# Key-value products of an attention kernel on 64x64 quarters of the array

## The chip, the cores and the metric

The kernel runs on one core of one Trainium2 chip. The metric is the device time of one execution in microseconds. Three executions of the kernel before took 288.51, 288.64 and 288.70 us; their median is 288.64.

## The reference

Eight batches of eight heads, 576 positions, head size 64, go through a linear attention: queries and keys each get a softmax of their own, keys and values are multiplied first, and a two-layer network follows.

```python
q_s = softmax(q, over the 64 features)
k_s = softmax(k, over the 576 positions)
kv  = einsum('bhsd,bhse->bhde', k_s, v)
a   = einsum('bhsd,bhde->bhse', q_s, kv)
x   = a, heads joined             # 4608 x 512
h   = x @ w_in                    # 512 x 2048
out = maximum(0.01 * h, h) @ w_out   # 2048 x 512
```

## The kernel before, in words

The 4608 rows are cut into nine tiles of 512 rows (`t` = 0 to 8), and the network runs tile by tile. For each tile `layer1` (L474) multiplies the transposed attention output `xT` by `w_in`, `leaky` (L483, ScalarE) writes the activations `gj`, `layer2` (L495) multiplies them by `w_out`, and `store` (L489) copies the result out and sends it. These matmuls use the whole array, 128 rows by 128 columns.

The attention of a batch is prepared while the network of earlier tiles runs. There is no scheduler: the order on each engine is the order of the program text. Small steps are hung on places of the network's loops by `at(t, u, ...)` and issued there by `run(t, u)`. So PE (TensorE) meets a batch's key-value products and its attention products at fixed places between the matmuls of the network. In stage 0, up to about 26 us, the steps for batch 0 are written out one after another, with `wake` matmuls of zeros between them, and PE has little else to do.

For one batch a tile of 128 partitions holds two heads at once: the partition number is 64 times the head's parity (`hh`) plus the block of positions, and each partition holds nine positions (`r` = 0 to 8) of four heads, `h` = 0 to 3 (`HL`). Thus every product over positions is a sum of nine matmuls with 64 rows each.

`v_cast` (L203 on ScalarE, L205 on GpSimd) writes the values as bf16 into `vb2`, beside a column of ones; the product of the keys' exponentials with that column is the sum by which the softmax of the keys is divided. `k_exp` writes the exponentials to `ke`.

`kv` (L287, batches 1 to 7) and `kv_pair` (L362, batch 0, in two halves) multiply. One matmul takes two heads at a time (`gg` is the pair): 64 rows, 128 columns of weights (two heads of 64 features), and 129 moving columns (two heads of 64 values, and the ones). Its output is 128 by 129, of which the two diagonal 64x64 blocks and the last column are used. The two parities `hh` are on the upper and the lower 64 rows of the array and write to different banks.

`kd_make` (L302 and L305) and, for batch 0, `kd_rec` (L373) and `kd_one` (L380) take the reciprocal of the sums and multiply the blocks with it into `kd2`, on VectorE, with one operation for each 64 partitions (`hp`), since the two blocks stand in different columns:

```python
for hp in range(2):
    rows = slice(hp * D, (hp + 1) * D)
    nc.vector.tensor_scalar(
        out=kd2[b % 2][rows, 2 * hh + gg],
        in0=pkv[rows, hp * D : (hp + 1) * D],
```

`quads` (L423), called by `attend` and `attend_x`, then multiplies the queries with `kd2` on 64x64 quarters of the array, and `move` copies the result to `xT` (L414, L416). The queries of batch 0 are turned by PE (`q_transpose`, L392, after `q_norm`, L272); those of later batches by a DMA (`q_turn`).

Of the kernel before, what the change touches and what calls it, by code (L numbers as in the profile page):

```python
# [8 lines left out]
FP32 = mybir.dt.float32  # L9
BF16 = mybir.dt.bfloat16  # L10
AF = mybir.ActivationFunctionType
ALU = mybir.AluOpType
# [7 lines left out]
L = 64  # L20
R = 9
HL = 4
# [3 lines left out]
def kernel(  # L26
# [9 lines left out]
    nc = tc.nc  # L36
# [3 lines left out]
    B, H, S, D = q.shape  # L40
# [6 lines left out]
    P = 128  # L47
# [7 lines left out]
    const_pool = ctx.enter_context(tc.tile_pool(name="const", bufs=1))  # L55
# [11 lines left out]
    psB_pool = ctx.enter_context(tc.tile_pool(name="psB", bufs=6, space=bass.MemoryType.PSUM))  # L67
    psO_pool = ctx.enter_context(tc.tile_pool(name="psO", bufs=2, space=bass.MemoryType.PSUM))
    BANK_TAG = "bank2k"


    def load(src, b, name, cuts):
# [15 lines left out]
    st = [{} for _ in range(B)]  # L88
# [7 lines left out]
        out=st[0]["q"][:, :, RB].rearrange("p h r d -> p h (r d)"),  # L96
        in_=qflat[:, :, RB].rearrange("p h r d -> p h (r d)"),
# [13 lines left out]
    w_out_sb = w_pool.tile([P, NF, O], BF16)  # L111
    xT = xT_pool.tile([P, NB, T], BF16)

    vb2 = [const_pool.tile([P, R, 2, 130], BF16, name=f"vb{i}") for i in range(2)]
    kd2 = [const_pool.tile([P, NB, D], BF16, name=f"kd{i}") for i in range(2)]
    for i in range(2):
        nc.gpsimd.memset(vb2[i][:, :, :, 128:129], 1.0)


    w_in_r = moe_w_in.rearrange("(c p) f -> p c f", p=P)  # L120
# [76 lines left out]
        )  # L197

    def v_cast(eng, b, gg):
        o = vb2[b % 2][:, :, gg, 0:128].rearrange("p r (h d) -> p h r d", h=2)  # L200
        i = st[b]["v"][:, 2 * gg : 2 * gg + 2]
        if eng is nc.scalar:
            eng.copy(out=o, in_=i)  # L203
        else:
            eng.tensor_copy(out=o, in_=i)  # L205
# [71 lines left out]
        )  # L277


    def kv(b):  # L280

        pkv = [psB_pool.tile([P, 2, 130], FP32, name="pkv", tag=BANK_TAG) for _ in range(2)]
        for gg in range(2):
            for r in range(R):
                for hh in range(2):
                    rows = slice(hh * L, (hh + 1) * L)
                    nc.tensor.matmul(  # L287
                        pkv[hh][:, gg, 0:129],
                        lhsT=st[b]["ke"][rows, r, 2 * gg : 2 * gg + 2].rearrange(
                            "p h d -> p (h d)"  # L290
                        ),
                        rhs=vb2[b % 2][rows, r, gg, 0:129],
                        start=(r == 0),
                        stop=(r == R - 1),
                    )
        st[b]["pkv"] = pkv

    def kd_make(b):
        for hh in range(2):
            pkv = st[b]["pkv"][hh]  # L300
            krec = small_pool.tile([P, 2, 1], FP32, name="krec")
            nc.vector.reciprocal(out=krec, in_=pkv[:, :, 128:129])  # L302
            for hp in range(2):
                p0 = hp * D
                nc.vector.tensor_tensor(  # L305
                    out=kd2[b % 2][p0 : p0 + D, 2 * hh : 2 * hh + 2],
                    in0=pkv[p0 : p0 + D, :, p0 : p0 + D],
                    in1=krec[p0 : p0 + D].to_broadcast([D, 2, D]),
                    op=ALU.mult,
                )  # L310

    wake_ps = psO_pool.tile([P, TT], FP32, name="pout")

# [41 lines left out]
        )  # L355

    def kv_pair(b, gg):
        pkv = [psB_pool.tile([P, 130], FP32, name="pkv1", tag=BANK_TAG) for _ in range(2)]
        for r in range(R):
            for hh in range(2):  # L360
                rows = slice(hh * L, (hh + 1) * L)
                nc.tensor.matmul(  # L362
                    pkv[hh][:, 0:129],
                    lhsT=st[b]["ke"][rows, r, 2 * gg : 2 * gg + 2].rearrange("p h d -> p (h d)"),
                    rhs=vb2[b % 2][rows, r, gg, 0:129],
                    start=(r == 0),
                    stop=(r == R - 1),
                )
        st[b]["pkv", gg] = pkv

    def kd_rec(b, gg, hh):
        st[b]["krec", gg, hh] = krec = small_pool.tile([P, 1], FP32, name="krec1")
        nc.vector.reciprocal(out=krec, in_=st[b]["pkv", gg][hh][:, 128:129])  # L373

    def kd_one(b, gg, hh):

        pkv, krec = st[b]["pkv", gg][hh], st[b]["krec", gg, hh]
        for hp in range(2):
            rows = slice(hp * D, (hp + 1) * D)
            nc.vector.tensor_scalar(  # L380
                out=kd2[b % 2][rows, 2 * hh + gg],
                in0=pkv[rows, hp * D : (hp + 1) * D],
                scalar1=krec[rows],
                scalar2=None,
                op0=ALU.mult,
            )

    def q_transpose(b, r0, n):
        ps = psB_pool.tile([P, NB, n, L], BF16, name="psum_qt", tag=BANK_TAG)
# [159 lines left out]
    k_exp(0, slice(0, 1))  # L549
    nc.gpsimd.tensor_copy(out=gate[:, 0:1], in_=st[0]["k"][:, 0, R - 1, D - 1 : D])  # L550
    v_cast(nc.gpsimd, 0, 1)
    k_all_dve(0, 1)
    k_all_pe(0, 1)
    wake(5)
    k_sub_ps(0, 0, HB)
    k_exp(0, slice(1, 2))
    v_cast(nc.scalar, 0, 0)
    k_sub_ps(0, 1)
    nc.gpsimd.tensor_copy(out=gate[:, 0:1], in_=st[0]["k"][:, HL - 1, R - 1, D - 1 : D])
    load_w_in(8, 16)  # L560
    k_exp(0, H1)
    q_first_rec(0, RA)
    q_norm(0, RA)
    kv_pair(0, 0)
    wake(1)
    q_transpose(0, 0, 4)
    kv_pair(0, 1)
    for hh in range(2):
        kd_rec(0, 0, hh)
        kd_one(0, 0, hh)  # L570
# [4 lines left out]
    q_sub(nc.gpsimd, 0, R1)  # L575
    q_keep(nc.vector, 0, 0, 4, (1,))
    kd_rec(0, 1, 0)
    kd_rec(0, 1, 1)
    kd_one(0, 1, 0)
    kd_one(0, 1, 1)  # L580
    q_exp(0, R1)
    q_max(0, R2)
# [18 lines left out]
    at(0, 15, lambda: k_sub(nc.vector, 1, H0), lambda: k_sub(nc.vector, 1, H1))  # L601
    at(0, 15, lambda: q_max(1, XR[1]), lambda: q_sub(nc.gpsimd, 1, XR[1]))
    at(0, 31, lambda: q_exp(1, XR[0]), lambda: k_exp(1, H0), lambda: v_cast(nc.scalar, 1, 0))
    at(0, 31, lambda: k_exp(1, H1), lambda: v_cast(nc.scalar, 1, 1), lambda: q_exp(1, XR[1]))
    at(0, 31, lambda: q_sum(1, XR[0]), lambda: q_norm(1, XR[0]))
    at(0, 34, lambda: q_turn(1, XR[0]))
    at(0, 39, lambda: kv(1), lambda: q_sum(1, XR[1]), lambda: q_norm(1, XR[1]), lambda: kd_make(1))
    at(0, 43, lambda: q_turn(1, XR[1]), lambda: load_all(2))
    for i in range(2):
# [6 lines left out]
    def plan(b, o):  # L616
        t = b - 2
        at(t, o, lambda: k_begin(b), lambda: q_begin(b), lambda: k_tree(b, ALLH))
        at(t, o + 3, lambda: k_allmax(b), lambda: k_sub(nc.gpsimd, b, ALLH))
        at(t, o + 7, lambda: q_max(b, ALLR), lambda: q_sub(nc.gpsimd, b, ALLR))  # L620
        at(t, o + 11, lambda: k_exp(b, ALLH))
        at(t, o + 12, lambda: v_cast(nc.gpsimd, b, 0), lambda: v_cast(nc.gpsimd, b, 1))
        at(t, o + 16, lambda: q_exp(b, ALLR))
        at(t, o + 18, lambda: q_sum(b, ALLR))
        at(t, o + 21, lambda: q_norm(b, ALLR))
        kvu, pu = o + 25, o + (33 if b == 3 else 34)
        at(t, kvu, lambda: kv(b))
        at(t, kvu + 1, lambda: kd_make(b))
        at(t, o + 22, lambda: q_turn(b))
        at(t, pu + 1, lambda: attend_x(b, (0, 1), (nc.scalar,)))  # L630


    def plan2():
        b = 2
        at(1, 0, lambda: k_begin(b), lambda: q_begin(b), lambda: k_tree(b, ALLH))
        at(1, 3, lambda: k_allmax(b))
        at(1, 6, lambda: k_sub(nc.vector, b, H0), lambda: k_sub(nc.vector, b, H1))
        at(1, 12, lambda: k_exp(b, ALLH))
        for rs in XR:
            at(1, 9, lambda rs=rs: q_max(b, rs), lambda rs=rs: q_sub(nc.gpsimd, b, rs))  # L640
        at(1, 13, lambda: v_cast(nc.gpsimd, b, 0), lambda: v_cast(nc.gpsimd, b, 1))
        for i, rs in enumerate(XR):
            at(1, (15, 16)[i], lambda rs=rs: q_exp(b, rs), lambda rs=rs: q_sum(b, rs), lambda rs=rs: q_norm(b, rs))
            at(1, (16, 17)[i], lambda rs=rs: q_turn(b, rs))
        at(1, 23, lambda: kv(b))
        at(1, 24, lambda: kd_make(b))
        for i in range(2):
            at(1, 28 + 2 * i, lambda i=i: attend_x(b, (i,), (nc.scalar,)))
# [121 lines left out]
```

## Time and profile before

| | us |
|---|---|
| median of three runs | 288.64 |
| profiled execution | 288.82 |
| span of its instructions | 287.0 |
| PE busy | 278.5 |
| VectorE busy | 150.5 |
| ScalarE busy | 146.0 |
| GpSimd busy | 82.3 |
| matmuls of `kv`, L287, 252 of them | 8.4 |
| `kd_make`, L305, 28 operations | 8.1 |
| `kd_one`, L380, 8 operations | 2.3 |

The profile is of one execution. PE is the matmul side of TensorE and PEld its weight loads, which overlap the matmuls; DVE is VectorE, ACT ScalarE, POOL GpSimd, SP the engine that issues most DMAs. A row of the groups names line, engine, operation, output and inputs, shapes and count, then busy time and the mean length of one. The length of a matmul in the profile is modelled and contains its passage through the array; how fast matmuls follow each other is read from their starts. The granted clock of TensorE was 1.00 throughout.

### The profile page before, as it was taken

To read this page: it belongs to the slowest core of one execution; us is meant where nothing else is said; L and a number is where in the kernel's file an instruction comes from. 1 tells how busy PE (TensorE), PEld (TensorE's weight loads), DVE (VectorE), ACT (ScalarE), POOL (GpSimd) and SP (SyncE) were. 2 spreads that over 40 slices of the span, in tenths; PEclk is the share of its full clock that TensorE was granted. 3 is DMA by queue.
4 is the path that set the end of the run, shared out by engine and by line. 5 is a ranking of instruction groups with operands and counts; after the bars stand their busy time and mean duration, and the time that the engine had idled before them with its cause. 6 is when DMAs were issued, how large, how long until landed. Compare 5 with 4: busy or idle time off the path is not lost.

```text
span 287.0 us, 4376 instructions
## 1 busy us (share of the span) xinstructions
PE 278.5 (97%) x1706; PEld 134.5 (47%) x1706; DVE 150.5 (52%) x250; ACT 146.0 (51%) x262; POOL 82.3 (29%) x61
## 2 busy tenths in 40 slices
PE   7699999999999999999999999999999999999995
PEld 2266744454444444454454444444454444444443
DVE  2997886896970994498185727563621100110011
ACT  4957890586269308923674358434843065016400
POOL 2522661017059009504900590049100000000000
PEclk9999999999999999999999999999999999999999
DMA  7999997999859174953398239913141310130032
GB/s 249 322 211 332 284 178 142 393 302 381 152 117 399 61 155 110 402 142 77 81 388 182 63 82 352 227 41 80 27 85 37 73 37 2 44 80 23 2 73 73
DMA packets 38868, 46.35 MB, mean 161 GB/s; under 512 B 18240, under 2 KB 21568, under 8 KB 38848
## 3 DMA queue, kind: packets, MB, share of 16 engines
q1 hardware_dynamic: 35456, 41.75, 49.8%
q0 software_dynamic: 3232, 4.19, 8.3%
q8 instruction: 13, 0.21, 0.3%
q10 hardware_dynamic: 160, 0.13, 0.1%
q14 instruction: 7, 0.06, 0.1%
HBM read 36.70 MB, written 9.44 MB: 161 GB/s over the span
## 4 chain that ended last, share of the span: by engine, by line
PE 91%; DVE 4%; issue 0%; ACT 0%
PE pout L495 44%; PE ph L474 42%; PE pkv L287 3%; PE po L423 2%; DVE kd L380 1%; DVE k_raw L353 1%; DVE qe L272 1%; DVE qmax L217 1%; DVE q_raw L248 0%; PE psum_qt L392 0%; DVE qT L410 0%; DVE qsum L265 0%; ACT qT L408 0%; DVE krec L373 0%; DVE out_sb L489 0%
## 5 line engine op out<-in xcount | busy, mean ns | idle before, releaser
L495 PE MATMUL pout<-w_out_sb,gj 128*128 128x512 bf16 (+2 forms) x592 | 127.9, 373 | 0.0
L474 PE MATMUL ph<-xT,w_in_sb 128*128 128x512 bf16 (+3 forms) x640 | 127.3, 358 | 0.0
L483 ACT ACTIVATE gj<-ph 128x512 bf16<-128x512 f32 (+2 forms) x152 | 83.3, 579 | 55.1 <-PE ph L474 53.3
L474 PEld LDWEIGHTS <-w_in_sb 128*128 128x128 bf16 x640 | 62.2, 98 | 62.1 <-issue 0.5
L495 PEld LDWEIGHTS <-gj 128*128 128x128 bf16 x592 | 56.3, 98 | 66.4 <-issue 1.9
L489 DVE COPY out_sb<-pout 128x512 f32<-128x512 f32 (+1 forms) x34 | 22.7, 675 | 83.6 <-PE pout L495 78.0
L185 POOL TENSOR_TENSOR k_raw<-k_raw,kall 128x2304 f32<-128x2304 f32 x5 | 25.3, 5066 | 75.7 <-DVE kall L177 45.4
L414 ACT CAST xT<-po 128x320 bf16<-128x320 f32 (+2 forms) x45 | 18.0, 486 | 47.8 <-PE po L423 47.8
L265 DVE TENSOR_REDUCE qsum<-qe 128x36 f32<-128x2304 bf16 (+4 forms) x11 | 19.8, 1798 | 32.1 <-ACT qe L256 32.1
L248 POOL TENSOR_TENSOR q_raw<-q_raw,qmax 128x2304 f32<-128x2304 f32 (+3 forms) x10 | 29.7, 2973 | 22.2 <-DVE qmax L217 22.2
L193 ACT ACTIVATE ke<-k_raw 128x2304 bf16<-128x2304 f32 (+2 forms) x11 | 17.5, 1595 | 11.1 <-POOL k_raw L185 10.9
L272 DVE TENSOR_TENSOR qe<-qe,qrec 128x2304 bf16<-128x2304 bf16 (+4 forms) x12 | 21.9, 1826 | 0.4
L217 DVE TENSOR_REDUCE qmax<-q_raw 128x36 f32<-128x2304 f32 (+4 forms) x11 | 19.6, 1792 | 0.5 <-DMA q_raw<-in_q_dram 0.5
L256 ACT ACTIVATE qe<-q_raw 128x2304 bf16<-128x2304 f32 (+4 forms) x11 | 16.8, 1525 | 3.1 <-POOL q_raw L248 1.7
L205 POOL CAST vb<-v_raw 128x1152 bf16<-128x1152 f32 x13 | 14.6, 1147 | 0.0
L152 DVE TENSOR_TENSOR t<-k_raw 128x1024 f32<-128x1024 f32 (+1 forms) x10 | 10.1, 1011 | 0.5 <-DMA k_raw<-in_k_dram 0.2
L316 PE MATMUL pout<-zero 128*128 128x512 bf16 x28 | 9.0, 450 | 1.3 <-POOL zero L101 1.3
L152 DVE TENSOR_TENSOR t<-t 128x256 f32<-128x256 f32 (+2 forms) x20 | 9.6, 478 | 0.7
L489 ACT COPY out_sb<-pout 128x512 f32<-128x512 f32 (+1 forms) x3 | 1.6, 544 | 14.1 <-PE pout L495 14.1
L287 PEld LDWEIGHTS <-ke 64*128 64x128 bf16 x252 | 7.1, 93 | 3.0 <-ACT gj L483 1.7
L305 DVE TENSOR_TENSOR kd<-pkv,krec 64x128 bf16<-64x128 f32 x28 | 8.1, 289 | 0.8
L287 PE MATMUL pkv<-vb,ke 64*128 64x129 bf16 x252 | 8.4, 216 | 0.0
(55 smaller groups left out, 91.5 us busy)
## 6 DMA issues: line engine op xcount, KB each, us to landing
out_dram<-out_sb SPq DMA_DIRECT2D x70, 128.0 KB, 2.4
q_raw<-in_q_dram SPq DMA_DIRECT2D x7, 1152.0 KB, 8.8
v_raw<-in_v_dram SPq DMA_DIRECT2D x7, 1152.0 KB, 11.6
k_raw<-in_k_dram SPq DMA_DIRECT2D x6, 1152.0 KB, 5.9
k_raw<-in_k_dram SPq DMA_DIRECT2D x4, 576.0 KB, 5.8
w_in_sb<-in_moe_w_in_dram POOLq DMA_DIRECT2D x4, 512.0 KB, 7.6
v_raw<-in_v_dram SPq DMA_DIRECT2D x2, 576.0 KB, 7.6
w_out_sb<-in_moe_w_out_dram POOLq DMA_DIRECT2D x4, 256.0 KB, 9.1
```

The source lines that it names most:

```text
L152: nc.vector.tensor_tensor(out=o, in0=i0, in1=i1, op=ALU.max)
L185: eng.tensor_tensor(out=ks, in0=ks, in1=st[b]["kall"][:, hs].unsqueeze(2).to_broadcast([P, n, R, D]), op=ALU.subtract,)
L217: nc.vector.tensor_reduce(out=m, in_=st[b]["q"][:, :, rs], axis=AX.X, op=ALU.max)
L248: eng.tensor_tensor(out=qs, in0=qs, in1=st[b]["qmax", rs.start].unsqueeze(3).to_broadcast([P, HL, n, D]), op=ALU.subtract,)
L265: nc.vector.reduce_sum(out=qsum, in_=st[b]["qe"][:, rs], axis=AX.X)
L272: nc.vector.tensor_tensor(out=qes, in0=qes, in1=st[b]["qrec", rs.start].unsqueeze(3).to_broadcast([P, n, HL, D]), op=ALU.mult,)
L287: nc.tensor.matmul(pkv[hh][:, gg, 0:129], lhsT=st[b]["ke"][rows, r, 2 * gg : 2 * gg + 2].rearrange("p h d -> p (h d)"), rhs=vb2[b % 2][row ...
L414: eng.copy(out=o, in_=i)
L474: nc.tensor.matmul(ph, lhsT=w_in_sb[:, i, j * P : (j + 1) * P], rhs=xT[:, i, c0 : c0 + n], start=(i == 0 and first), stop=(i == NB - 1 and ...
L483: nc.scalar.activation(out=o, in_=ph, func=AF.Prelu, alpha=LEAKY_SLOPE)
L489: copy(out=out_sb, in_=pout)
L495: nc.tensor.matmul(pout, lhsT=g_sb[j // 2][:, j % 2, tsub * P : (tsub + 1) * P], rhs=w_out_sb[:, j, os], start=(j == 0), stop=(j == NF - 1),)
```

## The change

Each key-value matmul now takes one head: 64 rows, 64 columns of weights, and 65 moving columns (the head's 64 values and a column of ones of its own). The two heads of a pair go to the two halves of the output's partitions, so that four matmuls, one for each quarter of the array, belong to each `r` and pair. A product of four pairs of heads is 72 matmuls and 72 weight loads instead of 36 and 36. All sums lie in one column, and both blocks in the same 64 columns, so one VectorE operation on 128 partitions divides what took two on 64. The rest of the program keeps its order on every engine.

```diff
-    vb2 = [const_pool.tile([P, R, 2, 130], BF16, name=f"vb{i}") for i in range(2)]
+    vb2 = [const_pool.tile([P, R, HL, 66], BF16, name=f"vb{i}") for i in range(2)]
...
-        nc.gpsimd.memset(vb2[i][:, :, :, 128:129], 1.0)
+        nc.gpsimd.memset(vb2[i][:, :, :, D : D + 1], 1.0)
...
-        o = vb2[b % 2][:, :, gg, 0:128].rearrange("p r (h d) -> p h r d", h=2)
+        o = vb2[b % 2][:, :, 2 * gg : 2 * gg + 2, 0:D].rearrange("p r h d -> p h r d")
...
-    def kv(b):
-
-        pkv = [psB_pool.tile([P, 2, 130], FP32, name="pkv", tag=BANK_TAG) for _ in range(2)]
-        for gg in range(2):
-            for r in range(R):
-                for hh in range(2):
-                    rows = slice(hh * L, (hh + 1) * L)
+    def kv_half(b, gg, outs):
+
+        for r in range(R):
+            for hh in range(2):
+                rows = slice(hh * L, (hh + 1) * L)
+                for hp in range(2):
                     nc.tensor.matmul(
-                        pkv[hh][:, gg, 0:129],
-                        lhsT=st[b]["ke"][rows, r, 2 * gg : 2 * gg + 2].rearrange(
-                            "p h d -> p (h d)"
-                        ),
-                        rhs=vb2[b % 2][rows, r, gg, 0:129],
+                        outs[hh][hp * D : (hp + 1) * D],
+                        lhsT=st[b]["ke"][rows, r, 2 * gg + hp],
+                        rhs=vb2[b % 2][rows, r, 2 * gg + hp, 0 : D + 1],
                         start=(r == 0),
                         stop=(r == R - 1),
                     )
+
+    def kv(b):
+        pkv = [psB_pool.tile([P, 2, 66], FP32, name="pkv", tag=BANK_TAG) for _ in range(2)]
+        for gg in range(2):
+            kv_half(b, gg, [p[:, gg, 0 : D + 1] for p in pkv])
         st[b]["pkv"] = pkv
...
             krec = small_pool.tile([P, 2, 1], FP32, name="krec")
-            nc.vector.reciprocal(out=krec, in_=pkv[:, :, 128:129])
-            for hp in range(2):
-                p0 = hp * D
-                nc.vector.tensor_tensor(
-                    out=kd2[b % 2][p0 : p0 + D, 2 * hh : 2 * hh + 2],
-                    in0=pkv[p0 : p0 + D, :, p0 : p0 + D],
-                    in1=krec[p0 : p0 + D].to_broadcast([D, 2, D]),
-                    op=ALU.mult,
-                )
+            nc.vector.reciprocal(out=krec, in_=pkv[:, :, D : D + 1])
+            nc.vector.tensor_tensor(
+                out=kd2[b % 2][:, 2 * hh : 2 * hh + 2],
+                in0=pkv[:, :, 0:D],
+                in1=krec.to_broadcast([P, 2, D]),
+                op=ALU.mult,
+            )
...
     def kv_pair(b, gg):
-        pkv = [psB_pool.tile([P, 130], FP32, name="pkv1", tag=BANK_TAG) for _ in range(2)]
...
+        pkv = [psB_pool.tile([P, 66], FP32, name="pkv1", tag=BANK_TAG) for _ in range(2)]
+        kv_half(b, gg, [p[:, 0 : D + 1] for p in pkv])
         st[b]["pkv", gg] = pkv
...
     def kd_one(b, gg, hh):
 
-        pkv, krec = st[b]["pkv", gg][hh], st[b]["krec", gg, hh]
-        for hp in range(2):
-            rows = slice(hp * D, (hp + 1) * D)
-            nc.vector.tensor_scalar(
-                out=kd2[b % 2][rows, 2 * hh + gg],
-                in0=pkv[rows, hp * D : (hp + 1) * D],
-                scalar1=krec[rows],
-                scalar2=None,
-                op0=ALU.mult,
-            )
+        nc.vector.tensor_scalar(
+            out=kd2[b % 2][:, 2 * hh + gg],
+            in0=st[b]["pkv", gg][hh][:, 0:D],
+            scalar1=st[b]["krec", gg, hh],
+            scalar2=None,
+            op0=ALU.mult,
+        )
```

More of the change, by code (lines that the diff above doesn't have):

```diff
@@ L357, in kv_pair @@
     def kv_pair(b, gg):
-        pkv = [psB_pool.tile([P, 130], FP32, name="pkv1", tag=BANK_TAG) for _ in range(2)]
[L359 to L367, printed above, removed]
-                )
+        pkv = [psB_pool.tile([P, 66], FP32, name="pkv1", tag=BANK_TAG) for _ in range(2)]
+        kv_half(b, gg, [p[:, 0 : D + 1] for p in pkv])
         st[b]["pkv", gg] = pkv
@@ L372, in kd_rec @@
         st[b]["krec", gg, hh] = krec = small_pool.tile([P, 1], FP32, name="krec1")
-        nc.vector.reciprocal(out=krec, in_=st[b]["pkv", gg][hh][:, 128:129])
+        nc.vector.reciprocal(out=krec, in_=st[b]["pkv", gg][hh][:, D : D + 1])
     def kd_one(b, gg, hh):
-        pkv, krec = st[b]["pkv", gg][hh], st[b]["krec", gg, hh]
-        for hp in range(2):
-            rows = slice(hp * D, (hp + 1) * D)
-            nc.vector.tensor_scalar(
-                out=kd2[b % 2][rows, 2 * hh + gg],
-                in0=pkv[rows, hp * D : (hp + 1) * D],
-                scalar1=krec[rows],
-                scalar2=None,
-                op0=ALU.mult,
-            )
+        nc.vector.tensor_scalar(
[5 more added lines that the diff above has]
+        )
     def q_transpose(b, r0, n):
```

## The prediction

> **What bounds the kernel now.** I read the page first: TensorE (PE) is busy nearly the whole span, and the chain that ended last runs through PE for 91% of it.
>
> ```profile
> PE 278.5 (97%) x1706; PEld 134.5 (47%) x1706; DVE 150.5 (52%) x250; ACT 146.0 (51%) x262; POOL 82.3 (29%) x61
> ...
> PE 91%; DVE 4%; issue 0%; ACT 0%
> PE pout L495 44%; PE ph L474 42%; PE pkv L287 3%; PE po L423 2%; DVE kd L380 1%; DVE k_raw L353 1%; DVE qe L272 1%; DVE qmax L217 1%; DVE q_raw L248 0%; PE psum_qt L392 0%; DVE qT L410 0%; DVE qsum L265 0%; ACT qT L408 0%; DVE krec L373 0%; DVE out_sb L489 0%
> ```
>
> The change touches two entries of this chain: the key-value products of batches 1 to 7 (L287, 3%), and in stage 0 the division on VectorE (DVE kd L380, 1%). Time taken from PE between 26 and 283 us is time off the span; VectorE counts only where PE waits for it, and that is in stage 0.
>
> One product of a later batch, from PE's timeline at 97.7 to 99.7 us (start, length, operation, count):
>
> ```profile
> 98.45 1.20 PE L287 MATMUL pkv<-vb,ke 64*128 64x129 bf16 x36
> 99.58 0.39 PE L495 MATMUL pout<-w_out_sb,gj 128*128 128x512 bf16 x1
> ```
>
> 36 matmuls and 36 weight loads take 1.13 us from the first matmul to the next one of another kind. In the trace they start in twos, 3 ns apart (the upper and the lower 64 rows of the array), and the twos follow every 56 ns, about 129 columns at full clock; the last starts 0.985 us after the first. Then 0.15 us pass until the next 128-row matmul starts: 54 ns of streaming and a gap of 92 ns, which the trace shows at each change of tile shape (L423 to L495 too).
>
> The same 64x64 quarters that the change wants are already used by L423. Its rows in the window 107.45 to 107.47 us, and the whole group:
>
> ```profile
> 107.45 0.11 PEld L423 LDWEIGHTS <-kd 64*64 64x64 bf16 x4 [0.42 <-issue]
> 107.45 0.33 PE L423 MATMUL po<-qX,kd 64*64 64x320 bf16 x4
> ...
> 107.45 0.68 PE L423 MATMUL po<-qX,kd 64*64 64x320 bf16 x16
> 108.07 0.39 PE L495 MATMUL pout<-w_out_sb,gj 128*128 128x512 bf16 x1
> ```
>
> Four matmuls of four quarters start within 10 ns, and the next four 136 ns later, which is 320 columns: four quarters do run side by side. The second four of a group come another 14 ns late, waiting for their weights.
>
> Stage 0, VectorE and then PE, from the timeline at 14 to 25 us:
>
> ```profile
> 14.46 0.60 DVE L380 TENSOR_SCALAR kd<-pkv,krec 64x64 bf16<-64x64 f32 x2
> 15.09 0.17 DVE L373 RECIPROCAL krec<-pkv 128x1 f32<-128x1 f32 x1
> 15.29 0.60 DVE L380 TENSOR_SCALAR kd<-pkv,krec 64x64 bf16<-64x64 f32 x2
> ...
> 17.18 1.23 DVE L380 TENSOR_SCALAR kd<-pkv,krec 64x64 bf16<-64x64 f32 x4
> ...
> 17.65 0.29 PE L423 MATMUL po<-qT,kd 64*64 64x256 bf16 x1
> 18.14 0.62 PE L423 MATMUL po<-qT,kd 64*64 64x256 bf16 x3 [0.20 <-DVE kd L380]
> 18.69 2.79 PE L474 MATMUL ph<-xT,w_in_sb 128*128 128x256 bf16 x24
> 22.00 0.40 PE L392 MATMUL psum_qt<-ident,qe 128*128 128x128 bf16 x4 [0.52 <-DVE qe L272]
> ```
>
> VectorE works here without a pause, and PE waits for it twice: the fourth L423 of this group starts at 18.46 instead of 17.66, because the last kd ended at 18.41 (0.80 us), and L392 sits idle for 0.52 us until qe of 21.95.
>
> **The change, part by part.**
>
> *Division, stage 0.* Eight kd operations of 283 ns become four. VectorE's time goes by columns, not partitions (128 columns take 292 ns on 128 partitions in L152, 289 ns on 64 in L305), so each stays near 0.28 us. With 31 ns between operations, 4 x (0.283 + 0.031) = 1.26 us leave VectorE's run between 14.46 and 21.95. PE can use all of it (0.80 + 0.52 = 1.32). What is late next is the second half of w_in, which landed at 23.10 and is first needed at 24.46, then 23.2: just in time. The query halves after that move with VectorE. I take -1.2 us.
>
> *Division, later batches.* 28 operations become 14 of the same 0.289 us, 128 columns each. They run beside PE, and L423 needs them 2 us later at the soonest (47.3 and 49.4 us in batch 1). Nothing.
>
> *Casts and ones.* The casts of V move the same 1152 elements per partition into runs of 66 instead of 130; the ones are 36 elements instead of 18 in two POOL memsets (0.19 us) before any load lands. Both are covered by waits of POOL for data, 5.5 us at the first gate. Nothing.
>
> *Products, the array's part.* Each product becomes 72 matmuls of 65 columns in 18 fours. A four streams in 65/129 of 56 ns, 28 ns; the quarter's weights, loaded behind the four before, take about 28 ns (the second set of L423's loads starts 28 ns after the first). With the 2 ns from a matmul's start to the next load, a four takes 30 to 32 ns. 17 x 30 + 14 + 27 + 92 + 3 ns = 0.65 us against 1.13: -0.48, or -0.45 at 32 ns. Seven products: -3.2 us. The shape changes remain and cost what they did.
>
> *Products, the issue part.* Half the columns are bought with twice the instructions, 144 a product instead of 72, and the array's pace asks for one each 4 ns. Nothing in the trace issues that fast for long. L423's fours are groups of 16 to 32 instructions that were queued while PE was busy. How many are queued: the sequencer's semaphore record at 62.60 us belongs to a weight load that ran at 66.04, and between the matmul then started and that load lie 33 instructions. While the head of the queue waits for a semaphore it is 16 (record at 14.42). So of 144 instructions 33 are ready and 111 must be issued while the product runs. What one costs no row shows; the bounds are:
> - from below, 1.6 ns, the spacing within L423's queued burst;
> - from above, 22 ns: the 36 instructions of kv_pair at 13.44 us began with 16 queued, and the 35th, a load, ran on time 0.418 us later;
> - one row of an empty queue, behind a semaphore record that ended at 6.245:
>
> ```profile
> 6.27 0.30 PEld L322 LDWEIGHTS pout<-nmax,identf 128*128 128x128 f32 x2 [0.84 <-issue]
> 6.30 0.36 PE L322 MATMUL pout<-nmax,identf 128*128 128x8 f32 x2 [0.38 <-DVE nmax L225]
> ```
>
> Here the matmul comes 31 ns after its load, while the same pair out of a filled queue (8.24 and 8.25) is 3 ns apart. That is one latency, not a rate, but it speaks for an issue nearer the upper end. I take 14 ns, the best that any long stretch of this trace sustains: 0.985 us for 35 matmuls with their loads. That is an estimate; the stretch itself was held by the array.
>
> 111 x 14 ns = 1.55 us to the last matmul against 0.985, less 27 ns for its shorter stream: +0.54 us a product, +3.8 us for seven. In stage 0 the two pairs also issue longer, but the first ends at about 14.23, some 0.05 us after VectorE would have taken its sums, and the second before VectorE asks for it.
>
> **Sum.** The profiled execution took 288.82 us (span 287.0 and 1.8 around it), 0.18 above the median of 288.64. 288.82 + 3.8 - 1.2 = 291.4; as a median 291.2. The break-even is 10.7 ns an instruction: there 111 x 10.7 exceeds 0.985 + 0.027 by 0.17, a seventh of 1.2.
>
> **Rivals.**
>
> *The array sets the pace* (issue under about 5 ns). For it: the bursts of L423, and that the 56 ns rhythm never stumbles. Against it: the 31 ns row. 288.82 - 3.2 - 1.2 = 284.4, median 284.2. Every issue cost below 10 ns lies between this and no change. Chance 0.36, and 0.10 for the stretch around the break-even (9 to 11 ns).
>
> *Each matmul has a slot of its own, and the queue does not help.* For it: averaged over a product, PE has started no matmul more often than every 28.1 ns, whether 129 columns are streamed or, in L423, 256. Against it: starts 3 ns apart. 71 x 28.1 ns = 2.0 us, +0.98 a product, +6.9 for seven; the first pair of stage 0 then also delays VectorE and leaves about 1.0 of the 1.2: 288.82 + 6.9 - 1.0 = 294.7, median 294.5. At the full 22 ns an instruction it would be 298. Chance 0.13. The Trainium skill (TensorEngine Tiling (Array Packing), Instruction Overhead) gives each matmul an overhead of some 60 cycles and advises against tiling along a dimension that is already small; at 25 ns, an estimate from that page, 72 slots would be 1.8 us. The trace's starts 3 ns apart disagree for a queued burst; no row here tests a long stream.
>
> **How the numbers follow.** Issue-bound with the queue helping: 0.41, the likeliest. Its own range, 11 to 17 ns, is 289 to 293.5. The range for all takes in the array's pace and the single slot: 283.7 to 296. Within 0.2% (0.58 us, what a measurement of this kernel can tell) lies about half of the 0.10 around the break-even, the rest of it on both sides: faster 0.36 + 0.03 = 0.39, same 0.05, slower 0.41 + 0.13 + 0.02 = 0.56.
>
> **What would show it.** In the product's timeline after: 72 matmuls over 1.5 to 1.7 us, the first fours 30 ns apart and, once the queue is empty, single loads and matmuls some 14 ns apart, would be the forecast; fours every 30 ns to the end and 0.65 us in all, the array; about 28 ns between matmuls from the start, the slot. In stage 0 the four kd operations at 0.28 us each and L392 at about 20.8 instead of 22.0 would show the division. If the product takes less than 1.0 us, or the division gains nothing, the forecast is wrong.

## The result, and the profile after

The changed kernel takes 285.12 us (284.66 to 285.36, four runs) against 288.59: a ratio of 0.9878, 95% interval 0.9861 to 0.9895. It is 3.5 us faster, where 2.6 us slower was forecast; the time lies inside the range, on the side of the first rival. The profiled execution took 284.93 us, its span 283.1, 3.9 less than before.

From the page of the changed kernel, the engines and the chain:

```profile
PE 272.0 (96%) x1967; PEld 131.4 (46%) x1994; DVE 143.6 (51%) x232; ACT 146.0 (52%) x262; POOL 82.7 (29%) x61
...
PE 86%; DMA 7%; issue 1%; DVE 1%; POOL 0%; SPq 0%; POOLq 0%
PE pout L483 44%; PE ph L462 38%; DMA w_out_sb<-in_moe_w_out_dram 3%; DMA w_in_sb<-in_moe_w_in_dram 2%; PE pkv L286 2%; DMA k_raw<-in_k_dram 2%; PE po L411 2%; DVE k_raw L353 1%; SPq L515 0%; POOL gate L580 0%; DVE out_sb L477 0%; POOL gate L547 0%; POOLq L580 0%; POOLq L547 0%
```

The products (now L286) fell from 3% to 2% of the chain and the kd operations of VectorE left it. New on it are three groups of DMAs: the head of the kernel now waits for loads. 27 of the 1994 matmuls have no record in this trace (the weight loads are complete), so PE's busy time is a little too low, and most of the "issue" in the chain stands where a record is missing.

PE's timeline at one product of a later batch:

```profile
41.61 0.38 PE L483 MATMUL pout<-w_out_sb,gj 128*128 128x512 bf16 x1
41.91 0.78 PE L286 MATMUL pkv<-vb,ke 64*64 64x65 bf16 x72
42.63 0.39 PE L483 MATMUL pout<-w_out_sb,gj 128*128 128x512 bf16 x1
```

72 matmuls with 72 loads take 0.71 us to the next matmul of another kind, in some products 0.74, against 1.13 for 36 before. The starts of the seven products stand 1.08, 1.50, 1.89, 2.28, 2.67, 3.07 and 3.49 us earlier than before: 1.08 us come from stage 0, and each product adds 0.40. Of the 1.08, 0.20 is not the change's: in this execution the first product of batch 0 already starts at 13.25 us, before at 13.45. Positions in stage 0 are therefore compared below as counted from that first product.

Stage 0, VectorE and then PE, timeline at 14 to 24 us and at 34 us:

```profile
14.06 0.16 DVE L364 RECIPROCAL krec<-pkv 128x1 f32<-128x1 f32 x1
14.26 0.28 DVE L368 TENSOR_SCALAR kd<-pkv,krec 128x64 bf16<-128x64 f32 x1
14.46 0.16 DVE L364 RECIPROCAL krec<-pkv 128x1 f32<-128x1 f32 x1
14.65 0.29 DVE L368 TENSOR_SCALAR kd<-pkv,krec 128x64 bf16<-128x64 f32 x1
14.85 0.68 DVE L217 TENSOR_REDUCE qmax<-q_raw 128x8 f32<-128x512 f32 x1
...
16.41 0.94 DVE L217 TENSOR_REDUCE qmax<-q_raw 128x12 f32<-128x768 f32 x1
...
17.38 0.30 PE L411 MATMUL po<-qT,kd 64*64 64x256 bf16 x4
17.62 2.79 PE L462 MATMUL ph<-xT,w_in_sb 128*128 128x256 bf16 x24
20.25 0.39 PE L380 MATMUL psum_qt<-ident,qe 128*128 128x128 bf16 x4
...
22.89 0.61 PE L462 MATMUL ph<-xT,w_in_sb 128*128 128x256 bf16 x4 [0.18 <-DMA w_in_sb<-in_moe_w_in_dram]
...
34.92 0.81 PE L483 MATMUL pout<-w_out_sb,gj 128*128 128x512 bf16 x2 [0.67 <-DMA w_out_sb<-in_moe_w_out_dram]
```

The four po matmuls at 17.38 run in one go, and the transposes at 20.25 no longer wait for VectorE. In exchange PE waits 0.18 us for the last piece of w_in and 0.67 us for the first piece of w_out.

The same places in the kernel before, VectorE and then PE:

```profile
14.26 0.16 DVE L373 RECIPROCAL krec<-pkv 128x1 f32<-128x1 f32 x1
...
18.44 0.95 DVE L217 TENSOR_REDUCE qmax<-q_raw 128x12 f32<-128x768 f32 x1
...
13.45 0.68 PE L362 MATMUL pkv<-vb,ke 64*128 64x129 bf16 x18 [0.80 <-ACT vb L203]
...
35.99 1.89 PE L495 MATMUL pout<-w_out_sb,gj 128*128 128x512 bf16 x8
```

Counted from the first product, the four transposes start at 8.55 us before and at 7.00 after; `layer2` starts at 22.54 before and, held by w_out, at 21.67 after.

### The profile page after: what moved, and what is told of

The parts are those of the page before. It is cut to its first block, busy times and chain, and to the rows that moved or that the text cites. A ratio compares the mean times of both kernels' runs of the same rounds, so it can differ in the third digit from the quotient of the medians.

```text
span 283.1 us, 4910 instructions
## 1 busy us (share of the span) xinstructions
PE 272.0 (96%) x1967; PEld 131.4 (46%) x1994; DVE 143.6 (51%) x232; ACT 146.0 (52%) x262; POOL 82.7 (29%) x61
## 4 chain that ended last, share of the span: by engine, by line
PE 86%; DMA 7%; issue 1%; DVE 1%; POOL 0%; SPq 0%; POOLq 0%
PE pout L483 44%; PE ph L462 38%; DMA w_out_sb<-in_moe_w_out_dram 3%; DMA w_in_sb<-in_moe_w_in_dram 2%; PE pkv L286 2%; DMA k_raw<-in_k_dram 2%; PE po L411 2%; DVE k_raw L353 1%; SPq L515 0%; POOL gate L580 0%; DVE out_sb L477 0%; POOL gate L547 0%; POOLq L580 0%; POOLq L547 0%
## 5 line engine op out<-in xcount | busy, mean ns | idle before, releaser
L483 PE MATMUL pout<-w_out_sb,gj 128*128 128x512 bf16 (+2 forms) x579 | 126.0, 373 | 2.0 <-issue 1.0
L316 PE MATMUL pout<-zero 128*128 128x512 bf16 x26 | 8.4, 453 | 1.3 <-POOL zero L101 1.3
L286 PEld LDWEIGHTS <-ke 64*64 64x64 bf16 x576 | 5.5, 106 | 4.4 <-ACT gj L471 1.7
L286 PE MATMUL pkv<-vb,ke 64*64 64x65 bf16 x576 | 6.5, 194 | 0.8 <-ACT vb L203 0.8
L230 ACT ACTIVATE qe<-q_raw,nmax 128x64 bf16<-128x64 f32 x16 | 5.3, 333 | 3.3 <-DVE nmax L225 3.3
```

The source lines that it names most:

```text
L286: nc.tensor.matmul(outs[hh][hp * D : (hp + 1) * D], lhsT=st[b]["ke"][rows, r, 2 * gg + hp], rhs=vb2[b % 2][rows, r, 2 * gg + hp, 0 : D + 1 ...
L483: nc.tensor.matmul(pout, lhsT=g_sb[j // 2][:, j % 2, tsub * P : (tsub + 1) * P], rhs=w_out_sb[:, j, os], start=(j == 0), stop=(j == NF - 1),)
```

## The experiments

All ratios are to the kernel before, on the chip of the run. `after_again`, the changed kernel once more, is the measure beside the first three experiments.

> The changed kernel once more beside the others: 284.7 to 285.4 in both theories, the spread following the landing of the first piece of w_out.

Measured: 285.19 us, ratio 0.9872 (0.9855 to 0.9890). In its profile PE waits 0.26 us for the first piece of w_out.

### Batch 0 as before, the later batches changed

Against the changed kernel; batch 0 gets a value tile of its own, `vb0`:

```diff
+        if b == 0:
+            o = vb0[:, :, gg, 0:128].rearrange("p r (h d) -> p h r d", h=2)
...
-        kv_half(b, gg, [p[:, 0 : D + 1] for p in pkv])
...
+                    rhs=vb0[rows, r, gg, 0:129],
...
+        for hp in range(2):
+            rows = slice(hp * D, (hp + 1) * D)
+            nc.vector.tensor_scalar(
```

> Batches 1 to 7 use the quarters, batch 0 keeps the 129-column products and the two division operations per half. Theory A (the products of the later batches and the division of batch 0 add up; a product costs PE 0.40 us less, VectorE's stage 0 gives the rest): seven products, -2.8 us, about 285.8. Rival B (most of the gain comes from stage 0, the products give theirs back later to loads or copies): 287.5 or more. Either way kv(1) starts at 43.0 us and kv(7) 2.4 us earlier than before under A.

Measured: 286.09 us, ratio 0.9900 (0.9884 to 0.9915), -2.8 us. From the first product of batch 0 to that of batch 1 it takes 29.53 us, as before (29.54); the seven products then save 0.40 us each, and nothing of it is given back up to the end. Theory A holds for the products.

### Only batch 0 changed

Against the kernel before, with a value tile of its own for batch 0 again:

```diff
-        pkv = [psB_pool.tile([P, 130], FP32, name="pkv1", tag=BANK_TAG) for _ in range(2)]
...
+        pkv = [psB_pool.tile([P, 66], FP32, name="pkv1", tag=BANK_TAG) for _ in range(2)]
+        kv_half(b, gg, [p[:, 0 : D + 1] for p in pkv])
```

> Only batch 0 uses the quarters and one division operation per half; batches 1 to 7 keep the 129-column products. Theory A: -1.1 us (0.7 to 1.1, as the first piece of w_out lands), about 287.6, with kv(1) at 41.9 us and a wait of PE for w_out_sb of some 0.7 us as in the changed kernel. Rival B: -2 us or more, 286.5 or less. Rival C (stage 0 is bound by loads alone, the division was worth nothing): no change, 288.6.

Measured: 288.32 us, ratio 0.9981 (0.9972 to 0.9990), -0.6 us. In its profile the product of batch 1 starts at 42.11 us, 0.88 us earlier than before, and PE waits where it waits in the changed kernel. PE's timeline at 34 us:

```profile
33.72 0.71 PE L482 MATMUL ph<-xT,w_in_sb 128*128 128x320 bf16 x4
35.12 0.81 PE L503 MATMUL pout<-w_out_sb,gj 128*128 128x512 bf16 x2 [0.69 <-DMA w_out_sb<-in_moe_w_out_dram]
```

The mechanism is that of theory A; its size is half of the 1.1 expected, and below its lower end of 0.7. The profile shows the fastest of the eleven runs (287.85 us, 0.97 below the profiled run of the kernel before), so it doesn't show what the slower ones lose; that stays open. B and C are both out.

### Quarters, but two division operations per half

```diff
-        nc.vector.tensor_scalar(
-            out=kd2[b % 2][:, 2 * hh + gg],
...
+        for hp in range(2):
+            rows = slice(hp * D, (hp + 1) * D)
+            nc.vector.tensor_scalar(
+                out=kd2[b % 2][rows, 2 * hh + gg],
```

(and the same in `kd_make`)

> The changed kernel, but each half is divided by two VectorE operations on 64 partitions again, in batch 0 and in the later ones. Theory A: products keep -2.8 us; VectorE in stage 0 is back to two operations of 0.283 us and 31 ns pauses, so about 285.8 and kv(1) at 43.0 us. Rival D (the shorter products of batch 0 give the gain of stage 0, not the division): the same as the changed kernel, 285.1, kv(1) at 41.9 us.

Measured: 286.17 us, ratio 0.9907 (0.9893 to 0.9922). The gain of stage 0 is gone: the product of batch 1 starts at 43.08 us, 29.54 after the first product as before, and the wait for VectorE is back. VectorE and PE of this kernel:

```profile
14.55 0.60 DVE L372 TENSOR_SCALAR kd<-pkv,krec 64x64 bf16<-64x64 f32 x2
15.19 0.17 DVE L366 RECIPROCAL krec<-pkv 128x1 f32<-128x1 f32 x1
15.39 0.60 DVE L372 TENSOR_SCALAR kd<-pkv,krec 64x64 bf16<-64x64 f32 x2
16.02 0.69 DVE L217 TENSOR_REDUCE qmax<-q_raw 128x8 f32<-128x512 f32 x1
...
22.09 0.40 PE L384 MATMUL psum_qt<-ident,qe 128*128 128x128 bf16 x4 [0.52 <-DVE qe L272]
```

So the division, not the shorter products of batch 0, gives what stage 0 gives; rival D falls. The two operations in the later batches cost nothing: from the product of batch 1 to the end this run takes 241.2 us, like the changed kernel. The pauses are seen too: here each kd pair ends before the next operation begins (16.02 after 15.99), while in the changed kernel qmax starts at 14.85 and kd runs until 14.94.

### What one instruction costs: the 65 columns in two parts

```diff
+        for cs in (slice(0, 33), slice(33, D + 1)):
...
-                        outs[hh][hp * D : (hp + 1) * D],
+                            outs[hh][hp * D : (hp + 1) * D, cs],
```

> The changed kernel with every quarter's 65 columns cut into 33 and 32: the same products from twice the instructions, 288 a product. Theory I (issue costs about 4.2 ns an instruction once the queue of some 33 is used up): the fours run faster at first, then the weight loads come evenly, 8.3 ns apart, a four every 33 ns; first to last matmul 1.05 to 1.2 us. Theory L (the quarter's weight load, some 30 ns, sets the four): fours of 30 to 32 ns with the four loads bunched 3 ns apart to the end, 1.1 us. Theory C (columns alone): a four every 17 ns, 0.6 us.

All parts of 33 columns of a pair come first, then those of 32, and each part loads its weights anew.

Measured, one execution: 292.86 us; first to last matmul of a product 1.17 to 1.31 us. For the first 25 fours or so they come every 31.7 ns, although each streams only half the columns. Their loads are bunched at first (3, 4 and 3 ns apart, then 21) and spread from the thirteenth four on; in the end they come evenly, 8 or 9 ns apart, and a four every 33.3 ns. Both theories are right, one after the other: while instructions are ready, a quarter needs 31.7 ns from one weight load to the next; when they run out, issue sets the pace, 33.3 ns for 8 instructions, 4.2 ns each. Columns alone (theory C) are out. That the weight load is what fills the 31.7 ns is argued, not shown: the first two loads of a quarter start 28 ns apart, but no run keeps the weights and repeats the matmul, so another fixed time of a quarter would look the same.

The changed kernel shows the same two phases: fours of 29 to 36 ns, 31.7 on average, then, in the second half of the product, loads 8 to 9 ns apart and fours of 31 to 32 on average. Issue and array are almost in balance at 65 columns.

The kernel loses more than its products cost. At 0.57 to 0.72 us more each, seven of them make 4.3 us. Another 4.1 us are lost behind the product of batch 5, as its PE timeline shows; together this is more than the 7.7 us between the two kernels, because in this execution the product of batch 1 starts 0.4 us earlier than in the changed kernel's profile.

```profile
149.31 0.51 PE L287 MATMUL pkv<-vb,ke 64*64 64x33 bf16 x38
149.75 1.68 PE L463 MATMUL ph<-xT,w_in_sb 128*128 128x512 bf16 x6
154.01 1.46 PE L463 MATMUL ph<-xT,w_in_sb 128*128 128x512 bf16 x3 [2.58 <-issue]
```

PE stands for 2.58 us and waits for nothing that the profile shows; the weight loads, whose records are complete, stand for 3.07. The instruction queue of the DMAs fetched a packet of 16 KB at 151.76 us, within 0.93 us, and another at 155.14; that PE had run out of instructions is argued from this, not shown. From 153.45 us the granted clock is 0.50 for 3.4 us, and the first matmuls behind the gap follow every 427 ns instead of 216. The changed kernel has no such gap.

### Two quarters at a time

```diff
-        for r in range(R):
-            for hh in range(2):
-                rows = slice(hh * L, (hh + 1) * L)
-                for hp in range(2):
+        for hp in range(2):
+            for r in range(R):
+                for hh in range(2):
+                    rows = slice(hh * L, (hh + 1) * L)
```

> The changed kernel with the order of the quarters changed: all matmuls of the left 64 columns of a pair of heads first, then those of the right, so that only two quarters run side by side; the same 144 instructions a product. Theory I: two quarters need 4 instructions, 17 ns, so the array sets the pace, 30 ns for a two, 36 twos, 1.05 us from first to last. If instead the issue cost were 14 ns, as the prediction took it, twos would come every 56 ns, 2.0 us.

Measured, one execution: 286.53 us; first to last matmul 0.854 us. PE's timeline:

```profile
96.98 1.04 PE L286 MATMUL pkv<-vb,ke 64*64 64x65 bf16 x72
98.19 0.38 PE L483 MATMUL pout<-w_out_sb,gj 128*128 128x512 bf16 x1 [0.16 <-issue]
```

The 0.16 us before the next matmul is again a missing record. From the second to the ninth two of a half they start every 32 ns on average, as the array was expected to allow (30 ns). The whole is shorter than the 1.05 us expected, because the halves overlap: a new two at 97.177 us starts while three twos of the nine before it are still to come. That it belongs to the next half is read from its length, 214 ns as for the first matmul of the product, and from the 53 ns to its second two, also as there. At 14 ns an instruction the product would take 2.0 us; that value is out a second time.

### The first piece of w_out, halved

```diff
-    for j0, j1 in ((0, 2), (2, 4), (4, 6), (6, 8), (8, 12), (12, 16)):
+    for j0, j1 in ((0, 1), (1, 2), (2, 4), (4, 6), (6, 8), (8, 12), (12, 16)):
```

In the changed kernel, and as a control in the kernel before:

> The changed kernel with the first piece of w_out halved, (0, 1) and (1, 2) instead of (0, 2). If the wait of 0.3 to 0.7 us of PE at its first use of w_out holds back what the division gained: the first layer2 starts at about 34.3 us without a wait, and the kernel takes 0.3 to 0.6 us less, 284.6. If the wait only hides another one behind it: 285.1, no change.

> The kernel before with the first piece of w_out halved in the same way. There PE reaches layer2 at 36.0 us, 1.8 us after the piece has landed, so both theories expect no change, 288.6 to 288.9.

Measured: 284.93 us, ratio 0.9860 (0.9845 to 0.9874), in the changed kernel; 288.84, ratio 0.9997 (0.9988 to 1.0006), in the kernel before. PE's timeline of the former at 34 to 37 us:

```profile
33.72 0.71 PE L462 MATMUL ph<-xT,w_in_sb 128*128 128x320 bf16 x4
34.26 1.89 PE L483 MATMUL pout<-w_out_sb,gj 128*128 128x512 bf16 x7
36.34 1.46 PE L483 MATMUL pout<-w_out_sb,gj 128*128 128x512 bf16 x6 [0.18 <-DMA w_out_sb<-in_moe_w_out_dram]
```

The first wait is gone and a smaller one has come behind it, 0.18 us for the piece `(2, 4)`, which lands at 36.29 us: each of the two theories holds in part. `layer2` starts 20.83 us after the first product of batch 0, the product of batch 1 at 41.61 us instead of 41.92, and the span is 282.7. It is the fastest kernel of the study, but its interval overlaps that of the changed kernel: 0.3 us of gain is likely, not settled.

## Why the prediction was wrong, point by point

- **What bounds the kernel: right.** Every 0.40 us taken from PE in a product is off the span. Nothing behind the products became late.
- **The array's part: right in kind, 0.05 to 0.08 us too good.** 0.65 to 0.68 us a product was worked out, 0.71 to 0.74 came. The fours come every 31.7 ns on average, as worked out (30 to 32). But the second four comes 53 ns after the first, not 44, and the last four is drawn out over some 25 ns, since its loads come evenly by then. The 44 came from a misreading: in the L423 group at 107.45 us the second four starts 160 ns after the first, 24 more than the 136 of the next, not 14. Seven products gave -2.8 us instead of -3.2. What sets the four was only half understood: not its columns (half of them changed nothing) but a time of 31.7 ns that a quarter needs from one weight load to the next.
- **The issue part: the step that failed.** The mechanism is there: a supply runs out, then instructions come at a fixed pace. Its price was taken as 14 ns and is 4.2, so 111 of them cost 0.46 us, less than the array takes, instead of 1.55. The forecast of +0.54 us a product became -0.40; a product under 1.0 us was its own sign of being wrong. The 14 ns came from a stretch that the array held at 56 ns a pair, which bounds the issue cost from above and says nothing else; and the 31 ns behind a semaphore record was a latency, which the text said and then weighed as a rate. Both rows allowed 4 ns as well as 14. That 33 instructions stand ready is not confirmed: the even loads set in after some 60 to 90. If 33 were ready, and the array took one each 4.0 ns (31.7 for 8) while 4.2 were needed for a new one, the supply would have lasted longer than the 144 of a product. How many are ready stays open.
- **The slot of each matmul: out.** 72 starts in 0.59 us are one every 8.2 ns. The Trainium skill (TensorEngine Tiling (Array Packing), Instruction Overhead) has some 60 cycles of overhead for each matmul and warns against tiling along a small dimension; as an engine-wide slot this is contradicted by these 8.2 ns.
- **Division, stage 0: the mechanism right, the sizes off, and -1.2 near by luck.** VectorE gained more than the 1.26 us worked out, 1.83 us from its first reciprocal to the second qmax (4.18 before, 2.35 after), since four operations of 0.28 and also the pauses around them are gone. The Trainium skill (VectorE: DVE Perf Modes, Two Vector instructions with no wait between them) gives as a model that an instruction whose input or output starts in another group of 32 partitions than the last one in the same memory starts only when every earlier one has finished. The trace agrees: 31 ns of pause after a kd on the upper 64 partitions, 80 ns of overlap after one on all 128.
- **Division, stage 0, what PE took of it.** PE gained more too: with the halved piece it reaches `layer2` 1.71 us earlier, counted from the first product (20.83 against 22.54), where 1.32 of waits had been listed. Without a wait there, the changed kernel would have reached it at 34.08; the first piece of w_out landed at 34.88 and took 0.84 of the 1.71 back (by starts; the row's 0.67 counts from the modelled end of the matmul before). The prediction named w_in as what is late next and did not weigh w_out, which in the profile before lay ready at 34.20, 1.8 us ahead of its use; in the kept profiles with the piece unhalved it lands between 34.12 and 35.07. So 0.9 us were left in this profile and 1.3 in that of `after_again`, and -1.2 is close because a gain that was counted too small met a wait that was not counted. In the whole kernel's time the division is worth 1.0 us (286.17 against 285.19).
- **Division in later batches, casts and ones: nothing, right.** From the product of batch 1 to the end the changed kernel takes 241.2 us against 244.0, which is the seven products' 2.8.

The sum as it came, in the profiled span: seven products -2.8, stage 0 -1.1 (1.71 less 0.84, and 0.20 from the earlier first product), together -3.9. The time lies 0.9 us above that of the first rival (284.2), whose terms -3.2 and -1.2 were each somewhat too large.

## What to carry to other kernels

A rate taken from a stretch that something else held back is only a bound. Here the bounds, 1.6 and 14 ns, lay on both sides of the break-even at 10.7, and the trace before had no long stretch held by issue alone; the likeliest value could not be read from it, and only the runs with the quarters measured it. More and smaller matmuls on quarters pay as long as the quarters run side by side and the burst stays short: 72 in fours took 0.71 to 0.74 us and 72 in twos 0.98, against 1.13 for the 36 before, but 144 took 1.28 to 1.43. At 8 instructions a four, issue (33.3 ns) and the quarter's own 31.7 ns are about even. And when an early stage gets faster, look for the next load in order of need, not only for the nearest one.

## What the runs showed of the hardware

- Weight loads and matmuls on 64x64 quarters came at 4.2 ns each in a long stretch (8 to 9 ns between loads).
- A 64x64 quarter took new weights every 31.7 ns on average, with 33 moving columns as with 65.
- Quarters do not wait for each other in program order: matmuls of the right half started with three twos of the left still to come.
- A VectorE operation on the upper 64 partitions was followed by 31 ns of pause, one on all 128 partitions by an operation that started some 80 ns before it ended.
- A product of 288 instructions in 1.2 us was followed once by 2.58 us in which PE stood idle, with an instruction fetch under way, and then by 3.4 us at a granted clock of 0.50. The cause is not shown.
